# Attention with a gated feed-forward: half-swapped rows copied a block ahead on POOL's queue, work moved to ACT at the start, and a rebuilt last part

## The chip, the cores and the metric

The kernel runs on one core of one Trainium2 chip. Five engines work side by side, each through its own instructions in order: PE (TensorE, matrix products; its weight loads, PEld, overlap with them), DVE (VectorE), ACT (ScalarE), POOL (GpSimd) and SP (SyncE, which issues transfers). SBUF is the memory on the core with 128 partitions; PSUM holds the matrix products in banks of 128 x 512 f32. Transfers (DMA) are issued from the queue of SP, ACT or POOL. An instruction on one engine that needs another's result waits on a semaphore.

The metric is the time of one execution in microseconds (us) on the device; shown is the median of three runs.

## What is computed

The reference, cut to what matters:

```python
def reference(A_x, A_k_cache, A_v_cache, A_wq, A_wo, B_x, B_w1, B_w3, B_w2):
    # x: 1 x 2048 x 640; k, v: 1 x 32 x 2048 x 192 (32 heads); wq: 640 x 6144; wo: 6144 x 640
    xn = (x - mean(x)) / sqrt(var(x) + 1e-5)             # per row
    q = (xn @ wq).reshape(1, 2048, 32, 192).transpose(0, 2, 1, 3)
    p = softmax(einsum("bhqd,bhkd->bhqk", q, k) * 192 ** -0.5)
    s = einsum("bhqk,bhkd->bhqd", p, v).transpose(0, 2, 1, 3).reshape(1, 2048, 6144) @ wo
    h = silu(xn @ w1) * (xn @ w3)                        # w1, w3: 640 x 1536
    g = silu(h @ w2)                                     # w2: 1536 x 640
    return x + s * g
```

All inputs and the output are bf16.

## The kernel before

The 2048 rows of x are 16 tiles of 128 rows (`NQT`) and 4 query blocks of 512 (`NQB`, index `qb`). Each head has 16 key tiles of 128, taken as 8 pairs (`NPAIR`, index `p`).

**Norm.** `ln_stats(i)` makes mean and variance of tile i on DVE (two batch statistics and an aggregate). `ln_sums` does the same for tile 1 alone on ACT: two passes with accumulators and a small scaling. `ln_root(i0)` makes the reciprocal roots of two tiles on ACT, `ln_scale(i0)` applies them on DVE. `ln_turn` transposes a pair of tiles on PE into a bank (`pst`) and copies them into `xnT` (ACT; DVE for tiles 2 and 3). `xnT` holds the normed x with its 640 columns on 5 x 128 partitions.

**Swapped rows.** `xnS` holds the same rows with the halves of the 128 partitions swapped, so that a product can be cut into two products of 64 rows that use both halves of PE at once. `swap_rows(qb)` (line 290) fills 512 columns of it with two transfers of 320 KB from `xnT`, issued on ACT's queue. `project_chunk(h, qb)` (line 260) makes a block of queries for head h: for head 0 from `xnT` alone, for all others from `xnT` and `xnS`. Its 512 x 2 product is cast into `qA` and `qF` (`cast`, on DVE unless given), and POOL makes shifted copies `qS` and `qD`. The chunk also carries a slice of w1 or w3, whose results are taken up by `swiglu_chunk` for most of the feed-forward's hidden part.

**Attention.** `advance(hd, qb, p, extra)` does one step: `scores` (6 products into an `st2` bank pair of `ps_st`, which has two), `weights` (one exp on ACT, 128 x 1024, with a bound `nb` instead of the row maximum), and the products of earlier steps with the values (`parts`, kept three half-steps behind; four when `extra` is given). `extra` is other PE work put between. After the last pair, `evict` copies and adds the halves of an output bank (`osum`, DVE), and writes the scaled result to `ostage`; for the second bank this last step is put off into `late`, which the next `advance` empties. The banks `ob0` and `ob1` are one each, so the next block's products wait until `osum` has left them.

**Head 0** runs interleaved with the rest of the norm: `extras` puts the transposes of the next block's tiles, head 0's own next projection and head 1's projection of the present block between the steps, `posts` puts statistics, roots and scalings behind them. In blocks 1 to 3 `swap_rows(qb)` follows step 0, and head 1's projection of that block, which reads it, comes at step 6 (block 3: step 1). POOL's weights for head 2 are issued at the start of block 3. `next_bound(qb)` makes the bound of the coming block: small DVE operations and an all-reduce over the partitions on POOL.

**Heads 1 to 31** project the next head's block at step 1 of each block. Head 31 has no next head: there `extra` calls `ffn_hidden(0, qb)` (line 514), which makes 128 hidden columns for 512 rows: ten products into an `st2` bank pair, tanh of the gate on ACT (`t`), and on DVE `a` = (t+1) * gate and `hT` = a * up, where gate and up are read from the two halves of the bank pair.

**Last part.** Ahead of the last two value parts of head 31 stands `ffn_hidden(1, 0)`. Then, for each block, the remaining hidden columns and four `ffn_out` (product with w2, tanh, gate into `g_all`); `tail_ps` hands out banks for both, in turn from `ps_st` and from `ob0`/`ob1`. Last come 16 `output_tile`: 96 products of 320 columns with wo (48 for each of two pieces of 320), a multiplication (`tmp`) and the sum with x (`res`) on DVE for each piece, and one store on ACT's queue. Only in the last tile are the two pieces made one after the other, in two banks. A branch behind it repeats everything exactly if a bound failed; it isn't taken.

`pin` keeps instructions of an engine in the order of the program.

Of the kernel before, what the change touches and what calls it, by code (L numbers as in the profile page):

```python
# [9 lines left out]
ACT = mybir.ActivationFunctionType  # L10
# [6 lines left out]
P = 128  # L17
# [13 lines left out]
def _kernel_impl(ctx, tc, A_x, A_k_cache, A_v_cache, A_wq, A_wo, B_w1, B_w3, B_w2, out):  # L31
# [96 lines left out]
    with ExitStack() as actx:  # L128
# [26 lines left out]
        sums = lnx.tile([P, 1], F32, name="sums")  # L155
        sqs = lnx.tile([P, 1], F32, name="sqs")
        nmean = lnx.tile([P, 1], F32, name="nmean")
# [27 lines left out]
        def ln_sums(i):  # L185
            junk = lnp.tile([P, D], BF16, tag="junk", name="junk")
            pin(nc.scalar.activation(out=junk[:], in_=x_all[:, i, :], func=ACT.Identity, accum_out=sums[:]))
            pin(nc.scalar.mul(out=nmean[:], in_=sums[:], mul=-1.0 / D))
            pin(nc.scalar.activation(out=junk[:], in_=x_all[:, i, :], func=ACT.Square, bias=nmean[:], scale=1.0,
                                     accum_out=sqs[:]))  # L190
# [3 lines left out]
        def ln_root(i0):  # L194
            lv = lnp.tile([P, 2], F32, tag="lv", name="lv")
            if i0 == 0:
                pin(nc.scalar.activation(out=lv[:, 0:1], in_=mv[:, 0, 1:2], func=ACT.Ln, bias=eps_t[:], scale=1.0))
                pin(nc.scalar.activation(out=lv[:, 1:2], in_=sqs[:], func=ACT.Ln, bias=eps_t[:], scale=1.0 / D))
            else:
                pin(nc.scalar.activation(out=lv[:].unsqueeze(2), in_=mv[:, i0:i0 + 2, 1:2], func=ACT.Ln, bias=eps_t[:],  # L200
                                         scale=1.0))
            rstd[i0] = lnx.tile([P, 2], F32, name=f"rstd{i0}")
            pin(nc.scalar.activation(out=rstd[i0][:], in_=lv[:], func=ACT.Exp, scale=-0.5))
# [3 lines left out]
        def ln_scale(i0):  # L207
            scaled[i0] = []
            for t in range(2):
                i = i0 + t  # L210
                xn = xnp.tile([P, D], BF16, tag="xn", name="xn")
                act = i == 1
                pin(nc.vector.tensor_scalar(out=xn[:], in0=x_all[:, i, :], scalar1=nmean[:] if act else mv[:, i, 0:1],
# [76 lines left out]
        def swap_rows(qb):  # L290
            qs = slice(qb * 512, (qb + 1) * 512)
            for t in range(2):
                pin(nc.scalar.dma_start(out=xnS[ROWS[t], :, qs], in_=xnT[ROWS[1 - t], :, qs]))
# [142 lines left out]
        maxima = project_chunk(0, 0, nc.scalar.copy)  # L436
        swap_rows(0)
# [8 lines left out]
        ln_stats(4)  # L446
# [8 lines left out]
        def first_project(h, qb):  # L455
            project_chunk(h, qb)()
# [3 lines left out]
        def steps(*fs):  # L460
# [4 lines left out]
            (0, 2): ((ln_root, 6), (ln_scale, 6)),  # L465
            (0, 3): ((ln_stats, 8), (ln_stats, 9)),
# [7 lines left out]
        for qb in range(NQB):  # L474
# [8 lines left out]
            for p in range(NPAIR):  # L483
                advance(heads[0], qb, p, extras.get(p), early.pop(0) if early else None)
                if p == 0 and qb:
                    swap_rows(qb)
# [30 lines left out]
        def ffn_hidden(qb, fl, ps):  # L517
# [7 lines left out]
            pin(nc.scalar.activation(out=t[:], in_=ps[:, 0:512], func=ACT.Tanh, scale=0.5))  # L525
            a = fsb.tile([P, 512], BF16, tag="a", name="a")
            pin(nc.vector.scalar_tensor_tensor(out=a[:], in0=t[:], scalar=1.0, in1=ps[:, 0:512], op0=ALU.add, op1=ALU.mult))  # L527
            pin(nc.vector.tensor_tensor(out=hT[:, FCP + fl, :], in0=a[:], in1=ps[:, 512:1024], op=ALU.mult))  # L528

        for h in range(1, H):  # L530
# [10 lines left out]
            for qb in range(NQB):  # L541
                post = []

                def extra():
# [5 lines left out]
                    else:  # L550
                        ffn_hidden(0, qb, ps_st.tile([P, 1024], F32, tag="st2", name="ps_gu"))
# [20 lines left out]
        def tail_ps(name):  # L572
            turn[0] += 1
            if turn[0] % 2:
                return ps_st.tile([P, 1024], F32, tag="st2", name=name)
            return ps_o.tile([P, 2, 512], F32, tag=f"ob{turn[0] // 2 % 2}", name=name)[:].rearrange("p t c -> p (t c)")
# [5 lines left out]
        ffn_hidden(1, 0, ps_st.tile([P, 1024], F32, tag="st2", name="ps_gu"))  # L582
        load_hT(1)
        while parts:
            parts.pop(0)()
        late.pop(0)()
# [18 lines left out]
    def output_tile(pools, i, oT, xt):  # L605
# [3 lines left out]
        pieces = [(ps_s[-pi if split else 0][:, pi * 512:pi * 512 + c1 - c0], c0, c1) for pi, (c0, c1) in enumerate(DP)]  # L609
# [10 lines left out]
        nc.scalar.dma_start(out=out2[i * P:(i + 1) * P, :], in_=res[:])  # L620
# [16 lines left out]
    with ExitStack() as dctx:  # L637
# [5 lines left out]
        for qb in range(NQB):  # L643
            if qb + 1 < NQB:
                for fl in range(1 if qb == 0 else 0, FC - FCP):
                    ffn_hidden(qb + 1, fl, tail_ps("ps_gu"))
# [139 lines left out]
```

## Time and profile before

| | |
|---|---|
| runs | 1965.85, 1967.06, 1969.59 us; median 1967.06 |
| the profiled execution | 1967.95 us; its span, first to last instruction, 1966.1 us |
| granted TensorE clock, mean over the span | 0.996 |
| DMA: queue of SP (q1), of ACT (q10), of POOL (q0) | 27.9%, 1.7%, 5.1% of 16 engines' span |
| exp of one step (L369, ACT) | 1016 + 8 of 1114 ns |
| query casts on DVE (L277, L278) / on ACT (head 0's first) | 691 and 681 ns / 585 and 592 ns |
| copy of a transposed tile (L222, ACT) | 694 ns |
| gate and product in `ffn_hidden` (L527, L528, DVE) | 687 and 687 ns |
| swap transfers (L293, ACT's queue) | 8 of 320 KB, median 5.5 us to landing |
| store of a result tile (L620, ACT's queue) | 16 of 160 KB, median 8.7 us to landing, 1.8 at least |

How to read it: a busy time is the sum of an engine's instructions; PE's products overlap one another a little in these records. A wait is time in which an engine stood idle before an instruction, put down to what ended it. A line of the timeline gives start, duration, engine, line, operation, output <- inputs, shapes, count, and in brackets the idle time before it with what ended it. "Landing" is when a transfer's semaphore is complete, counted from the start of its issue.

### The profile page before, as it was taken

The numbers are of one execution on the slowest core, as the hardware profiler recorded it, in microseconds if no ns is written. First come the engines' busy times: TensorE is split into PE (matmuls) and PEld (weight loads), VectorE is DVE, ScalarE is ACT, GpSimd is POOL, SyncE is SP. The second block draws the span as 40 slices with busy tenths as digits, with TensorE's granted clock in tenths as the row PEclk, the third lists the DMA queues.
The fourth block names the chain that finished last, engine by engine and source line by source line (L and its number), as shares of the span: only waits on it lengthen the run. The fifth ranks groups of instructions, "written<-read, shape, count | busy, mean of one in ns | idle before, by whom it ended". The sixth has DMA issues, their size and how long they took to land.

```text
span 1966.1 us, 60463 instructions
## 1 busy us (share of the span) xinstructions
PE 1940.3 (99%) x27233; PEld 1422.1 (72%) x27233; DVE 1140.2 (58%) x2256; ACT 1213.7 (62%) x1176; POOL 435.5 (22%) x632
## 2 busy tenths in 40 slices
PE   8899999999999999999999999999999999999998
PEld 4577777777777777777777766666666666567776
DVE  7666667666666666666666666666666653421111
ACT  5577767677777777777777777777777777210000
POOL 2322222222222222222222222222222110000000
PEclk9999999999999999999999999999999999999999
DMA  9322323222233322232323232323232112927882
GB/s 207 64 68 48 68 53 69 58 62 64 62 68 62 68 62 68 54 88 68 75 54 76 54 76 48 82 46 84 46 84 46 39 42 84 269 58 139 154 155 51
DMA packets 354681, 153.51 MB, mean 78 GB/s; under 512 B 303648, under 2 KB 348160, under 8 KB 354416
## 3 DMA queue, kind: packets, MB, share of 16 engines
q1 hardware_dynamic: 337200, 117.82, 27.9%
q0 software_dynamic: 8032, 23.93, 5.1%
q10 hardware_dynamic: 9184, 7.83, 1.7%
q8 instruction: 215, 3.52, 0.8%
q14 instruction: 50, 0.41, 0.1%
HBM read 56.23 MB, written 31.98 MB: 45 GB/s over the span
## 4 chain that ended last, share of the span: by engine, by line
PE 96%; DVE 2%; DMA 1%; ACT 0%; issue 0%; POOL 0%; SPq 0%; ACTq 0%
PE obank L409 34%; PE st L363 33%; PE ps L275 14%; PE ps_s L612 11%; PE ps_f L628 3%; PE ps_gu L522 2%; PE ps L269 0%; DVE st L182 0%; DMA xnS<-xnT 0%; DVE st L286 0%; ACT pT L369 0%; DMA x_all<-in_A_x_dram 0%; DVE a L527 0%; DVE hT L528 0%; DVE osum L380 0%
## 5 line engine op out<-in xcount | busy, mean ns | idle before, releaser
L369 ACT ACTIVATE pT<-st,nb 128x1024 bf16<-128x1024 f32 x1016 | 1131.4, 1114 | 455.7 <-PE st L363 454.1
L409 PEld LDWEIGHTS <-pT 64*128 64x128 bf16 x16384 | 762.5, 94 | 196.0 <-DVE osum L380 2.5
L409 PE MATMUL obank<-vt,pT 64*128 64x193 bf16 x16384 | 876.9, 243 | 2.6 <-DVE osum L380 2.1
L379 DVE COPY osum<-obank 128x386 f32<-128x386 f32 x256 | 142.5, 556 | 506.5 <-PE obank L409 506.5
L363 PE MATMUL st<-qA,KA 64*128 64x512 bf16 x2048 | 415.3, 376 | 4.7 <-ACT pT L369 2.5
L363 PE MATMUL st<-qS,KB 64*128 64x512 bf16 x1024 | 385.2, 376 | 0.3 <-POOL qS L281 0.3
L363 PE MATMUL st<-qS,KC 64*128 64x512 bf16 x1024 | 385.0, 376 | 0.3 <-POOL qS L281 0.3
L363 PE MATMUL st<-qD,KC 64*128 64x512 bf16 x1024 | 385.0, 376 | 0.3 <-POOL qD L282 0.3
L363 PE MATMUL st<-qF,KB 64*128 64x512 bf16 x1024 | 385.0, 376 | 0.0
L281 POOL COPY qS<-qA 64x512 bf16<-64x512 bf16 x256 | 190.9, 746 | 604.4 <-DVE qA L277 595.5
L275 PE MATMUL ps<-xnT,wq 64*128 64x512 bf16 x1240 | 292.2, 378 | 0.0
L275 PE MATMUL ps<-xnS,wq 64*128 64x512 bf16 x1240 | 284.7, 378 | 5.8 <-DMA xnS<-xnT 5.8
L363 PEld LDWEIGHTS <-KC 64*128 64x128 bf16 x2048 | 191.9, 94 | 97.1 <-issue 1.4
L275 PEld LDWEIGHTS <-wq 64*128 64x128 bf16 x2480 | 146.7, 94 | 100.8 <-issue 8.1
L612 PE MATMUL ps_s<-wo_sb,oT 128*128 128x320 bf16 x1536 | 208.8, 299 | 0.0
L363 PEld LDWEIGHTS <-KB 64*128 64x128 bf16 x2048 | 192.5, 94 | 13.2 <-issue 0.8
L612 PEld LDWEIGHTS <-oT 128*128 128x128 bf16 x1536 | 150.3, 98 | 58.3
L386 DVE TENSOR_TENSOR ostage<-osum,rl_all 128x384 bf16<-128x384 f32 x256 | 149.6, 584 | 8.8
L380 DVE TENSOR_TENSOR osum<-osum,obank 128x386 f32<-128x386 f32 x256 | 142.6, 557 | 8.9
L363 PEld LDWEIGHTS <-KA 64*128 64x128 bf16 x2048 | 126.8, 94 | 21.0 <-issue 8.8
L617 DVE SCALAR_TENSOR_TENSOR tmp<-ps_s,g_all 128x320 f32<-128x320 f32 x32 | 15.6, 488 | 176.4 <-PE ps_s L612 176.4
L277 DVE CAST qA<-ps 128x512 bf16<-128x512 f32 x127 | 87.8, 691 | 37.7 <-PE ps L275 13.6
(85 smaller groups left out, 1175.4 us busy)
## 6 DMA issues: line engine op xcount, KB each, us to landing
vt<-in_A_v_cache_dram SPq DMA_DIRECT2D x32, 768.0 KB, 6.4
o_scr<-ostage SPq DMA_DIRECT2D x64, 384.0 KB, 2.9
wo_sb<-in_A_wo_dram POOLq DMA_DIRECT2D x1, 7680.0 KB, 33.1
wq<-in_A_wq_dram POOLq DMA_DIRECT2D x31, 160.0 KB, 3.0
hT_scr<-hblk SPq DMA_DIRECT2D x16, 256.0 KB, 2.9
xnS<-xnT ACTq DMA_DIRECT2D x8, 320.0 KB, 5.5
xt<-in_A_x_dram POOLq DMA_DIRECT2D x16, 160.0 KB, 9.5
out_dram<-res ACTq DMA_DIRECT2D x16, 160.0 KB, 8.7
```

Source lines behind the costliest of these rows:

```text
L275: pin(nc.tensor.matmul(ps[:, t * 512:(t + 1) * 512], lhsT=wq[ROWS[t], s, :], rhs=xs[ROWS[t], s // 2, qs], start=(s == 0), stop=(s == 2 * D ...
L277: pin(cast(out=qA[:, qs], in_=ps[:, 0:512]))
L281: keep(nc.gpsimd.tensor_copy(out=qS[ROWS[t], qs], in_=qA[ROWS[1 - t], qs]))
L363: pin(nc.tensor.matmul(st2[:, t * 512:(t + 1) * 512], lhsT=k[ROWS[t], ks], rhs=q[ROWS[t], qs], start=(s == 0), stop=(s == 2)))
L369: pin(nc.scalar.activation(out=pT2[:], in_=st2[:], func=ACT.Exp, scale=SCALE, bias=nb[:]))
L379: pin(nc.vector.tensor_copy(out=osum[:], in_=ov[:, 0, :, 0:DH + 1]))
L380: pin(nc.vector.tensor_tensor(out=osum[:], in0=osum[:], in1=ov[:, 1, :, 0:DH + 1], op=ALU.add))
L386: pin(nc.vector.tensor_tensor(out=ostage[:, b * 2:b * 2 + 2, hg * DH:(hg + 1) * DH], in0=osum[:, :, 0:DH], in1=rl.unsqueeze(2).to_broadcas ...
L409: pin(nc.tensor.matmul(acc["o"][b][:, r, (j % 2) * 256:(j % 2) * 256 + DH + 1], lhsT=pT2[ROWS[r], t * 512 + j * P:t * 512 + (j + 1) * P], ...
L522: pin(nc.tensor.matmul(ps[:, o:o + 512], lhsT=w_sb[:, c, fl * P:(fl + 1) * P], rhs=xnT[:, c, qs], start=(c == 0), stop=(c == DC - 1)))
L612: pin(nc.tensor.matmul(ps, lhsT=oT[:, k, :], rhs=wo_sb[:, k, c0:c1], start=(k == 0), stop=(k == OC - 1)))
L628: pin(nc.tensor.matmul(ps[:, pi * 512:pi * 512 + c1 - c0], lhsT=hT[:, fc, qsl], rhs=w2_sb[:, fc, c0:c1], start=(fc == 0), stop=(fc == FC - ...
```

## The change

In the start:

- `swap_rows` issues on POOL's queue. Block 0 is swapped where it was in the program; blocks 1 to 3 are swapped one block ahead, behind step 5 of block 0 and step 4 of blocks 1 and 2.
- The statistics of tile 4 move from DVE (`ln_stats(4)`) to ACT (`ln_sums(4)`, behind head 0's first casts); the sums have two columns now, and `ln_root` takes the logarithm of the pair 4, 5 in two instructions.
- `ln_root(6)` and `ln_scale(6)` come behind step 3 of block 0 instead of step 2.
- Head 1's four projections are cast by ACT instead of DVE.

In `ffn_hidden`: DVE first copies the up half of the bank pair to SBUF (`u`, bf16); the product `hT` = a * u is returned as a function. Head 31 calls it from `late`, behind the put-off eviction; the one ahead of the last two value parts is called behind them; the others at once.

In the last part: `tail_ps` gives the second tail tile a bank pair of `ps_st` instead of `ob1`, and from there on even turns `ps_st`, odd turns `ob0` and `ob1` in turn. The last output tile is cut into 512 and 128 columns instead of 320 and 320, and each piece is stored by itself.

```diff
+        ASUM = {1: 0, 4: 1}
...
         def ln_sums(i):
+            k = slice(ASUM[i], ASUM[i] + 1)
...
-            pin(nc.scalar.activation(out=junk[:], in_=x_all[:, i, :], func=ACT.Identity, accum_out=sums[:]))
+            pin(nc.scalar.activation(out=junk[:], in_=x_all[:, i, :], func=ACT.Identity, accum_out=sums[:, k]))
...
         def ln_root(i0):
-            if i0 == 0:
...
+            if i0 in ASUM or i0 + 1 in ASUM:
+                for t in range(2):
+                    i = i0 + t
+                    if i in ASUM:
+                        pin(nc.scalar.activation(out=lv[:, t:t + 1], in_=sqs[:, ASUM[i]:ASUM[i] + 1], func=ACT.Ln, bias=eps_t[:],
+                                                 scale=1.0 / D))
+                    else:
+                        pin(nc.scalar.activation(out=lv[:, t:t + 1], in_=mv[:, i, 1:2], func=ACT.Ln, bias=eps_t[:], scale=1.0))
...
         def swap_rows(qb):
...
-                pin(nc.scalar.dma_start(out=xnS[ROWS[t], :, qs], in_=xnT[ROWS[1 - t], :, qs]))
+                pin(nc.gpsimd.dma_start(out=xnS[ROWS[t], :, qs], in_=xnT[ROWS[1 - t], :, qs]))
...
         maxima = project_chunk(0, 0, nc.scalar.copy)
+        ln_sums(4)
         swap_rows(0)
...
-        ln_stats(4)
         ln_stats(5)
...
         def first_project(h, qb):
-            project_chunk(h, qb)()
+            project_chunk(h, qb, nc.vector.tensor_copy if h == 0 else nc.scalar.copy)()
...
-            (0, 2): ((ln_root, 6), (ln_scale, 6)),
-            (0, 3): ((ln_stats, 8), (ln_stats, 9)),
+            (0, 3): ((ln_root, 6), (ln_scale, 6), (ln_stats, 8), (ln_stats, 9)),
...
                 advance(heads[0], qb, p, extras.get(p), early.pop(0) if early else None)
-                if p == 0 and qb:
-                    swap_rows(qb)
+                if p == (4 if qb else 5) and more:
+                    swap_rows(qb + 1)
...
             pin(nc.scalar.activation(out=t[:], in_=ps[:, 0:512], func=ACT.Tanh, scale=0.5))
+            u = fsb.tile([P, 512], BF16, tag="u", name="u")
+            pin(nc.vector.tensor_copy(out=u[:], in_=ps[:, 512:1024]))
             a = fsb.tile([P, 512], BF16, tag="a", name="a")
             pin(nc.vector.scalar_tensor_tensor(out=a[:], in0=t[:], scalar=1.0, in1=ps[:, 0:512], op0=ALU.add, op1=ALU.mult))
-            pin(nc.vector.tensor_tensor(out=hT[:, FCP + fl, :], in0=a[:], in1=ps[:, 512:1024], op=ALU.mult))
+            return lambda: pin(nc.vector.tensor_tensor(out=hT[:, FCP + fl, :], in0=a[:], in1=u[:], op=ALU.mult))
...
-                        ffn_hidden(0, qb, ps_st.tile([P, 1024], F32, tag="st2", name="ps_gu"))
+                        late.append(ffn_hidden(0, qb, ps_st.tile([P, 1024], F32, tag="st2", name="ps_gu")))
...
             turn[0] += 1
-            if turn[0] % 2:
+            if turn[0] == 1 or turn[0] % 2 == 0:
                 return ps_st.tile([P, 1024], F32, tag="st2", name=name)
-            return ps_o.tile([P, 2, 512], F32, tag=f"ob{turn[0] // 2 % 2}", name=name)[:].rearrange("p t c -> p (t c)")
+            return ps_o.tile([P, 2, 512], F32, tag=f"ob{(turn[0] // 2 + 1) % 2}", name=name)[:].rearrange("p t c -> p (t c)")
...
-        ffn_hidden(1, 0, ps_st.tile([P, 1024], F32, tag="st2", name="ps_gu"))
+        rest = ffn_hidden(1, 0, ps_st.tile([P, 1024], F32, tag="st2", name="ps_gu"))
         load_hT(1)
         while parts:
             parts.pop(0)()
+        rest()
         late.pop(0)()
...
-        pieces = [(ps_s[-pi if split else 0][:, pi * 512:pi * 512 + c1 - c0], c0, c1) for pi, (c0, c1) in enumerate(DP)]
+        pieces = [(ps_s[-pi if split else 0][:, pi * 512:pi * 512 + c1 - c0], c0, c1)
+                  for pi, (c0, c1) in enumerate(((0, 512), (512, D)) if split else DP)]
...
-        nc.scalar.dma_start(out=out2[i * P:(i + 1) * P, :], in_=res[:])
+            if split:
+                nc.scalar.dma_start(out=out2[i * P:(i + 1) * P, c0:c1], in_=res[:, c0:c1])
+        if not split:
+            nc.scalar.dma_start(out=out2[i * P:(i + 1) * P, :], in_=res[:])
...
-                    ffn_hidden(qb + 1, fl, tail_ps("ps_gu"))
+                    ffn_hidden(qb + 1, fl, tail_ps("ps_gu"))()
```

## The prediction

> **What bounds the kernel now.** I read the page's busy times, the chain of waits, PE's waits, the stretches around the two long ones, and the timeline.
>
> ```profile
> span 1966.1 us, 60463 instructions
> PE 1940.3 (99%) x27233; PEld 1422.1 (72%) x27233; DVE 1140.2 (58%) x2256; ACT 1213.7 (62%) x1176; POOL 435.5 (22%) x632
> PE 96%; DVE 2%; DMA 1%; ACT 0%; issue 0%; POOL 0%; SPq 0%; ACTq 0%
> ```
>
> PE is the bound: 1940.3 of 1966.1 us. Heads 1 to 30 run the same instructions in the same order on every engine in both kernels, and PE's waits below all lie before 81 us or after 1616. So the change can only move the 25.8 us in which PE stands still, and stretches in which PE is busy but slow. PE's waits over the span, the largest:
>
> ```profile
> PE ps L275 <- DMA xnS<-xnT: 5.8, 1, 5.8
> PE st L363 <- ACT pT L369: 2.5, 4, 1.7
> PE obank L409 <- DVE osum L380: 2.1, 2, 1.5
> PE ps_gu L522 <- DVE osum L380: 2.0, 1, 2.0
> PE st L363 <- DVE hT L528: 1.5, 4, 0.4
> ```
>
> (us in total, times, longest.) The stretches (us, then busy time of PE, PEld, DVE, ACT, POOL; granted clock; DMA share; GB/s) show a second cost behind two of these waits:
>
> ```profile
> 75.00:80.00 5.00, 0.00 (x0) 0.00 (x0) 2.85 (x6) 1.11 (x1) 2.84 (x4) 0.81 0.78 161
> 80.00:85.00 5.00, 4.73 (x24) 1.98 (x25) 0.27 (x1) 0.00 (x0) 0.01 (x1) 0.51 0.00 0
> 1672.00:1676.00 4.00, 1.98 (x9) 0.72 (x8) 3.79 (x9) 0.60 (x1) 0.00 (x0) 0.94 0.00 0
> 1675.50:1680.00 4.50, 4.50 (x14) 1.71 (x15) 1.99 (x4) 0.45 (x1) 0.00 (x0) 0.62 0.62 135
> ```
>
> After the 5.8 us wait PE runs at half clock up to 84.9; after the 2.0 us wait it does so too, from 1675.5 on. The 1.7 us wait (at 21.9) and the 1.5 us one (at 39.3) show no such drop.
>
> **(a) Swapped rows one block earlier, on POOL's queue.** Before, block 3's swap is issued on ACT at 73.41 and PE wants it at 74.3:
>
> ```profile
> 68.73 0.38 POOL L322 PARTITION_ALL_REDUCE nb<-ns  x1 [0.55 <-DVE ns L319]
> 71.20 1.27 POOL L281 COPY qS<-qA 64x512 bf16<-64x512 bf16 x2 [2.09 <-DVE qA L277]
> 73.41 1.79 ACTq L293 DMA_DIRECT2D xnS<-xnT  x1
> 80.27 0.61 PE L275 MATMUL ps<-xnS,wq 64*128 64x512 bf16 x2 [5.79 <-DMA xnS<-xnT]
> ```
>
> The wait costs 5.8 us. The half clock from 80.27 to 84.9 costs half of 4.6, so 2.3; together 8.1. In the new POOL order block 3's two transfers stand right behind the all-reduce that ends at 69.11, in the 2.09 us where POOL idled. An issue on POOL takes 0.72 to 1.04 us (rows of wq), so the two take about 1.5 and qS waits at most 0.1 longer; behind qS stand qD, weights and KC of later heads, not wanted before 88. In the other blocks KC or qS of head 1 stand behind the swap, wanted no sooner. Queue SP's order is unchanged, and ACT loses eight issues. Landing is not shown for this copy on this queue. The same copy on ACT's queue, alone at 54.8, landed its halves 3.6 and 4.6 us after issue: 69.85+4.6 = 74.45 against 74.3. Loads on POOL's queue took 2.4 to 3.0 alone, 4.7 to 5.7 beside the swap at 73, and 10.3 to 10.8 in the crowded start. So 0 to 6 us of waiting remain; I take 0.4, because the stretch 69 to 74 moves only 3 GB/s and resembles 54.8 most. Gain 7.7.
> Blocks 1 and 2 have over 9 us between landing and use. Block 0 goes from ACT (12.79) to POOL behind qD (15.3), ahead of head 1's weights, and is wanted near 31.7. Those weights, issued at 15.24, landed 10.5 us later; up to 22.3 the DMA view lists 0.65 MB of the swap's queue and no packet of POOL's. That same 0.65 MB now precedes the weights in POOL's own queue, so I expect them at 27.3 as before and cost it at nothing; at the 0.33 MB per 3.4 us that POOL's queue made from 22.3, both would land near 33, a wait of 1.5.
> The row: the 62 wq issues of POOL average 737 ns against 716 at best, though DVE is 58% busy. The Trainium skill (SBUF — State Buffer, section "SBUF: two separate sides") warns that a DMA from the GpSimd queue can stall while DVE holds the shared port in a two-port mode, and sends such transfers to ACT or SP; by that rule the two issues could be stretched, which is the first rival. That row does not bear it out.
>
> **(b) Tile 4's statistics on ACT, head 1's first casts on ACT, root 6 one step later.** Tile 4's sums take 2.02 us on ACT (4.04 to 6.06 for tile 1). x tile 4 lands at 14.2 (issue 8.84, 5.4 us), so ACT ends at 16.3, before the first exp at 17.21: hidden, margin 0.9.
>
> ```profile
> 23.58 0.39 PE L363 MATMUL st<-qA,KA 64*128 64x512 bf16 x2 [1.73 <-ACT pT L369]
> ...
> 40.86 1.01 PE L409 MATMUL obank<-vt,pT 64*128 64x193 bf16 x20 [1.52 <-DVE osum L380]
> ```
>
> DVE loses two batch statistics and an aggregate, 1.1 us. Before, exp 3 stood behind root 6, which waited for DVE until 22.00, and PE idled 1.7. Now exp 3 starts near 20.9, but two copies (1.3) and the root (0.5) come before exp 4, and the transposes of tile 6 wait for its rstd until 24.35 instead of 25.00: 0.65 gained. The three-instruction root instead of two costs ACT 0.2, hidden.
> Head 1's casts leave DVE (0.69+0.68) and cost ACT 1.07 a time. ACT idled 2.0 before the next exp in these steps, so that exp slips 0.3 and PE, three half-steps ahead, does not see it. DVE reaches the eviction of the finished block 0.5 earlier. At 37.6 PE gains that; the 1.5 us osum wait at 40.86 moves with it and stays (bounds of the whole 0 to 1.8). I take 1.0. At 58.8 a wait of 0.5 shrinks, while exp at 57.3 may slip 0.1: 0.3 (bounds -0.3 to 0.8).
>
> **(c) ffn_hidden with the copy u.** In head 31 PE's four 0.37 us waits are for hT, the second reader of the bank: t 0.60, a 0.69, hT 0.69 in a row. Now u (0.69, as a cast of 512) runs beside t, and the bank is free after a: 0.6 us earlier. All four go: 1.5.
>
> **(d) Tail order.**
>
> ```profile
> 1675.50 6.17 PE L522 MATMUL ps_gu<-xnT,w_sb 128*128 128x512 bf16 x20 [2.02 <-DVE osum L380]
> ```
>
> The second tail tile now takes the st2 bank that ffn_hidden(1,0) frees near 1671.95 instead of ob1, free at 1675.46. PE wants it at 1673.4: 2.0 gained, and the half clock: 20 matmuls took 6.17 us where 40 take 8.7 later, so 1.8. DVE adds u but hT from SBUF should fall toward 0.42 (hblk row), some 1.8 a chunk against PE's 2.16. The next st2 bank is freed near 1677.55, wanted at 1677.8: narrow. Gain 3.85 (0 to 3.9).
>
> **(e) Last tile 512+128.**
>
> ```profile
> 1959.87 0.49 DVE L617 SCALAR_TENSOR_TENSOR tmp<-ps_s,g_all 128x320 f32<-128x320 f32 x1 [5.50 <-PE ps_s L612]
> 1960.40 0.49 DVE L619 TENSOR_TENSOR res<-tmp,xt 128x320 bf16<-128x320 f32 x1
> 1960.92 0.34 ACTq L620 DMA_DIRECT2D out_dram<-res  x1
> ```
>
> Matmuls: 48 of 512 columns at 0.215 (L522) and 48 of 128 at 0.057 (transposes of L221: 10 in 0.73, less one's 0.22, over 9) make 13.07 against 13.04; were each held by its 98 ns weight load, +2.0. DVE: 320 columns 0.49, 512 columns 0.69, so 128 take 0.29: -0.4. The store landed 3.4 us after issue, others of its size in 1.8 at best; a fifth of the bytes: -0.4 (0 to -1.6). Gain 0.8 (-1.6 to 2).
>
> **Sum.** 7.7+1.0+0.3+1.5+3.85+0.8 = 15.15 us. The profiled execution took 1967.95 (1.85 around its span) and becomes 1952.8; the median shown, 1967.06, lies 0.9 lower, so 1952.
>
> **Rivals.**
> 1. The swap of block 3 still comes late. If each issue on POOL is held by one DVE cast (0.69), or first packets start 1.2 later as beside other traffic (4.7 against 3.6 landed), 2 us of waiting return, and with them a half-clock stretch like the tail's 1.8: 1952+1.6+1.8 = 1955.5. For: 74.45 against 74.3 is no margin. Against: little other traffic then.
> 2. Block 0 and head 1's weights land near 33: 1.5 lost, 1953.5; with half clock 1955.5.
> 3. The tail's wait turns into one for DVE: nothing of (d) is gained, 1955.9. For: margin 0.25. Against: PE would wait for only one a, 0.7.
> 4. Other residual waits near 1.7 us lose the clock. The drop lasted 3.4 us after 2.0 us of idling and 6.8 after 5.8. The Trainium skill (TensorE: Matmul & The Clock Gate, section "What's actually happening") has a free-running window of about 3.4 us, with half rate after an idle one; the trace agrees with the length, but shows a drop after 2.0 us. So the osum wait near 39.7 could cost 1.7: 1953.7.
> 5. Slower: POOL's queue serves its five transfers of the start one after another, each with the 5.7 us beyond the usual that its first showed (7.1 to the first packet against 1.4). Head 1's last weights then land near 45 against 31.7: 13 lost, 2.3 of clock, and (a) is lost too, 8: 1976. It decides from 15 us lost. Against: the three landed within 2.2 us of each other.
>
> **Chances.** Forecast 0.55 (own range 1949.5 to 1954.5); rival 1 0.15, rival 2 0.08, rival 3 0.08, rival 4 0.06, rival 5 0.06, nothing net 0.02. Within 0.2% (3.9 us, what a measurement can tell) lies only the last. Range 1947.5 to 1958.5: the lower end is (b) and (e) at their good bounds, the upper rivals 1 and 3 together. Faster 0.92, same 0.02, slower 0.06.
>
> **What would show it.** PE's wait for xnS under 0.5 us and a clock of 1.00 from 72 to 90; no PE wait for hT in head 31; no PE wait for osum and clock 1.00 near 1672; DVE's last two at 0.29. A wait for xnS or wq above 2 us, or one for `a` in the tail, makes me wrong.

## The result, and where the time went

The changed kernel takes 1961.05 us (median of 7 runs, 1956.17 to 1963.59), the kernel before 1967.78 in the same set (1965.56 to 1971.42): ratio 0.996, 95% interval 0.9947 to 0.9973. By the medians it is faster by 6.7 us and not by the 15.15 forecast, and it lies 2.55 us above the range. The execution whose profile is shown next took 1956.17 and is the fastest of the seven; the page's span, busy times and chain:

```profile
span 1954.4 us, 60484 instructions
PE 1938.0 (99%) x27233; PEld 1329.0 (68%) x27233; DVE 1139.2 (58%) x2261; ACT 1219.5 (62%) x1190; POOL 439.5 (22%) x640
PE 97%; DVE 1%; DMA 1%; ACT 0%; POOL 0%; issue 0%; DVEq 0%
```

PE is still the bound. Its waits (us in total, times, longest):

```profile
PE pst L228 <- DVE xn L220: 2.8, 3, 1.9
PE obank L416 <- DVE osum L387: 2.1, 3, 1.5
...
PE st L370 <- DVE a L535: 1.0, 4, 0.3
```

Gone are the 5.8 us for the swapped rows, the 1.7 at 21.9 and the tail's 2.0. The four waits of head 31 are still there, 0.25 each in place of 0.37. The stretches that answer to those of before (PE, PEld, DVE, ACT, POOL; granted clock; DMA share; GB/s):

```profile
75.00:80.00 5.00, 4.78 (x60) 2.70 (x56) 4.80 (x9) 3.07 (x4) 4.84 (x8) 1.00 0.35 76
80.00:85.00 5.00, 5.00 (x88) 3.74 (x86) 3.86 (x10) 4.08 (x4) 2.91 (x5) 1.00 0.22 58
...
1664.50:1671.00 6.50, 6.50 (x34) 2.96 (x31) 6.27 (x14) 1.19 (x2) 0.00 (x0) 1.00 0.05 15
```

PE works through both places at full clock. I compared the start times of the same products in both traces, group by group. Of the 11.7 us by which this span is shorter, 7.7 come between 68 and 100 us (block 3's swap), 0.65 from the first block, 0.5 from head 31, 3.87 from the second tail tile, 1.17 from the end. 1.5 are lost again before 12 us (a half clock from 7.7 to 11.1 us that the profile of before does not have) and 0.8 in small steps between 100 and 1610 us; I have no cause for the latter.

So this one execution has nearly all that was forecast. What the other six lost, 3 to 7 us, is not in it. Two more executions of the same kernel show it, in the first experiment.

### The profile page after: what moved, and what is told of

Same layout as the page of the kernel before. It is cut to its first block, busy times and chain, and to the rows that moved or that the text cites. A ratio compares the mean times of both kernels' runs of the same rounds, so it can differ in the third digit from the quotient of the medians.

```text
span 1954.4 us, 60484 instructions
## 1 busy us (share of the span) xinstructions
PE 1938.0 (99%) x27233; PEld 1329.0 (68%) x27233; DVE 1139.2 (58%) x2261; ACT 1219.5 (62%) x1190; POOL 439.5 (22%) x640
## 4 chain that ended last, share of the span: by engine, by line
PE 97%; DVE 1%; DMA 1%; ACT 0%; POOL 0%; issue 0%; DVEq 0%
PE obank L416 34%; PE st L370 33%; PE ps L282 14%; PE ps_s L622 11%; PE ps_f L641 3%; PE ps_gu L528 2%; DMA wq<-in_A_wq_dram 1%; PE ps L276 0%; DVE st L293 0%; DVE osum L387 0%; DMA x_all<-in_A_x_dram 0%; DVE osum L386 0%; DVE xn L220 0%; DVE u L533 0%; DVE ostage L393 0%
## 5 line engine op out<-in xcount | busy, mean ns | idle before, releaser
L416 PEld LDWEIGHTS <-pT 64*128 64x128 bf16 x16384 | 718.4, 94 | 240.4 <-DVE osum L387 2.8
L416 PE MATMUL obank<-vt,pT 64*128 64x193 bf16 x16384 | 855.2, 243 | 2.6 <-DVE osum L387 2.1
L370 PE MATMUL st<-qA,KA 64*128 64x512 bf16 x2048 | 392.5, 376 | 2.7 <-DVE a L535 1.0
L622 PE MATMUL ps_s<-wo_sb,oT 128*128 128x320 bf16 (+2 forms) x1536 | 208.8, 299 | 0.0
L282 PEld LDWEIGHTS <-wq 64*128 64x128 bf16 x2480 | 122.5, 94 | 115.3 <-DMA wq<-in_B_w_dram 0.6
L370 PEld LDWEIGHTS <-KA 64*128 64x128 bf16 x2048 | 104.9, 93 | 21.7 <-issue 6.7
L627 DVE SCALAR_TENSOR_TENSOR tmp<-ps_s,g_all 128x320 f32<-128x320 f32 (+2 forms) x32 | 15.6, 487 | 176.1 <-PE ps_s L622 176.1
L99 POOL DMA_DIRECT2D wq<-in_A_wq_dram x62 | 45.2, 730 | 278.0 <-PE ps L282 265.8
```

Of the source, the lines that this page charges most:

```text
L99: keep(nc.gpsimd.dma_start(out=wq[ROWS[t], :, c0:c1], in_=w.rearrange("(s p) d -> p s d", p=DT)))
L282: pin(nc.tensor.matmul(ps[:, t * 512:(t + 1) * 512], lhsT=wq[ROWS[t], s, :], rhs=xs[ROWS[t], s // 2, qs], start=(s == 0), stop=(s == 2 * D ...
L370: pin(nc.tensor.matmul(st2[:, t * 512:(t + 1) * 512], lhsT=k[ROWS[t], ks], rhs=q[ROWS[t], qs], start=(s == 0), stop=(s == 2)))
L416: pin(nc.tensor.matmul(acc["o"][b][:, r, (j % 2) * 256:(j % 2) * 256 + DH + 1], lhsT=pT2[ROWS[r], t * 512 + j * P:t * 512 + (j + 1) * P], ...
L622: pin(nc.tensor.matmul(ps, lhsT=oT[:, k, :], rhs=wo_sb[:, k, c0:c1], start=(k == 0), stop=(k == OC - 1)))
```

## Experiments

Every time is the median of its runs; "before" is the kernel before in the same set (1967.2 to 1967.8 in all sets).

**The change once more, twice (look_a, look_b).** No edit.

> The changed kernel again, for a second profile: its seven times spread from 1956.17 to 1963.59 us and the profiled one was the lowest. Theory: in the profiled one PE reached head 1's first projection late, because a half-clock stretch at 7.7 to 11.1 us had cost it 1.5 us, and so it waited only 0.2 us for head 1's weights, which land near 33 us behind the swap of block 0 in POOL's queue. In a run without that stretch PE comes at about 31.2 us and waits 1.5 to 2.5 us there, with a half-clock stretch behind the wait: span 1957 to 1960. Rival: no wait above 0.5 us there, and the time is lost in half-clock stretches that follow no such wait.

> The same kernel a third time; the same two expectations as for the second look. If the theory holds, the wait for weights or swapped rows near 32 us grows by as much as PE comes earlier, in each of the looks.

Measured: 1960.94 and 1964.35. All their loss against the profile above arises between 27 and 43 us (5.8 and 9.5 us in the start times of the products); behind it the three executions keep their distance. PE's timeline of look_a there:

```profile
31.09 0.24 PE L416 MATMUL obank<-vt,pT 64*128 64x193 bf16 x1
35.12 0.80 PE L416 MATMUL obank<-vt,pT 64*128 64x193 bf16 x7 [3.78 <-issue]
```

PE stops for 3.78 us behind the first of eight equal value products, and the releaser is "issue": nothing that the profile shows held it. Its inputs come from the same two tiles as those of the product before it. The stretches of look_a show what follows:

```profile
30.00:35.00 5.00, 1.33 (x23) 0.74 (x18) 3.73 (x11) 1.88 (x2) 3.48 (x6) 0.91 1.23 92
35.00:40.00 5.00, 4.88 (x29) 3.43 (x30) 0.00 (x0) 0.00 (x0) 1.03 (x1) 0.50 1.14 239
```

The clock is half in the second line. The DMA engines are taken all the time (share above 1) and yet move only 92 GB/s in the first. Look_a has no wait for head 1's weights: the theory had the place and the half clock, but not the cause. Look_b stops at the same product for 1.7 us and then does wait for them, by more than the 2 us that the prediction named as a sign of being wrong:

```profile
PE ps L282 <- DMA wq<-in_A_wq_dram: 5.5, 2, 4.9
PE obank L416 <- issue: 1.7, 1, 1.7
```

**Block 0's swap back on ACT, at its new place (swap0_act), and the early swaps alone (only_swap).**

The first edits the change, the second the kernel before (`swap_rows` takes the engine as an argument in the first):

```diff
-        swap_rows(0)
+        swap_rows(0, nc.scalar)
```
```diff
-                pin(nc.scalar.dma_start(out=xnS[ROWS[t], :, qs], in_=xnT[ROWS[1 - t], :, qs]))
+                pin(nc.gpsimd.dma_start(out=xnS[ROWS[t], :, qs], in_=xnT[ROWS[1 - t], :, qs]))
...
-                if p == 0 and qb:
-                    swap_rows(qb)
+                if p == (4 if qb else 5) and more:
+                    swap_rows(qb + 1)
```

> The changed kernel with block 0's swap alone issued on ACT's queue again. Theory (head 1's weights stand behind the swap in POOL's queue): the weights land near 27 us as before the change, PE does not wait near 32 us, and the median falls 3 to 5 us under the changed kernel's 1961.05, to 1956 to 1958 us. Rival (the spread comes from the clock alone, in the start or the tail): no gain, 1960 to 1962 us.

> The kernel before with the swap alone changed: POOL's queue, one block ahead. Theory: the wait at 74 us and its half clock go, 7.8 us, and a wait of 1 to 2 us for head 1's weights near 32 us is added, with or without 1.7 us of half clock: 1960.5 to 1963 us. Rival (no cost at 32 us): 1959 to 1960.5 us. Rival (the gain at 74 us is given back later): above 1964 us.

Measured: swap0_act 1955.61 (1954.94 to 1961.09), ratio 0.9943 (0.993 to 0.9956); only_swap 1964.63 (1961.34 to 1971.57), ratio 0.9992 (0.998 to 1.0003).

Swap0_act's median is even a little under what was expected, but not for the reason given: in its profile (1959.42) head 1's weights land at 33.0 to 35.1 us and not near 27. Its five times fall into two groups, 1954.94 to 1955.61 (three) and 1959.42 and 1961.09. So with the swap late but on ACT's queue most of the loss is absent in three executions of five; none of these was profiled, and why is open.

Only_swap is the part of the change that was to bring 7.7 us. Made alone it brings 3.0 by the medians, and the interval of its ratio includes no gain at all. Its profile gains 7.3 us between 68 and 100 us and has lost 5.4 between 31 and 38.

Both profiled executions have the stop, 2.2 and 3.3 us at the same product, and a half clock behind it; in swap0_act too, although its swap is not on POOL's queue. What the two share with the change is the late issue of block 0's swap: 16.5 us on ACT, since it now stands behind tile 4's statistics, 15.4 to 16.7 on POOL, where it stands behind the copies of head 0's queries; before, 12.8.

**What PE waits for.** Queue q8 ("instruction" in the page's list of queues) carries packets of 16 KB. The table gives, for each profiled execution, when block 0's swap and head 1's first key transposes were issued, the first such packet of the trace (the expectation of act_early calls it the second), and the product at which PE stopped, the second of those eight (us, worked out from the traces' records):

```
                 swap issued    keys    q8 packet      product   behind its  PE stood
                 (queue)        issued  from - to      starts    landing     still
before           12.8 (ACT)     15.9    23.27-24.54    31.77      7.2        -
the change       16.7 (POOL)    15.1    28.88-30.82    32.38      1.56       -
look_a           15.4 (POOL)    15.7    32.68-33.72    35.12      1.40       3.8
look_b           15.4 (POOL)    15.4    29.65-31.53    33.02      1.49       1.7
swap0_act        16.5 (ACT)     15.4    32.52-33.57    35.00      1.43       2.2
only_swap        15.5 (POOL)    15.2    32.88-34.00    35.49      1.50       3.3
before_pool0     15.7 (POOL)    16.2    32.23-34.20    35.59      1.39       3.1
keys_wait        17.1 (POOL)    15.6    33.96-34.99    36.27      1.28       2.4
act_early        12.9 (ACT)     16.8    24.20-25.48    31.95      6.5        -
swap0_sp         15.4 (SP)      16.9    27.99-29.00    32.65      3.6        -
pool_early       12.0 (POOL)    16.6    28.01-29.02    35.63      6.6        -
keys_wait2       15.5 (POOL)    25.6    24.00-25.21    31.10      5.9        -
act_early_junk   13.1 (ACT)     16.2    24.36-25.64    31.23      5.6        -
```

In every execution that stops, the product starts 1.3 to 1.5 us after that packet has landed; where the packet is earlier, nothing stops. The three other profiled executions (no_u, no_b, fills14, below) agree: landed 3.2 to 7.9 us ahead of the product, no stop. I read this as PE running out of program: the packet brings its next instructions. The trace does not name the engine a packet is for, so this is inferred. The counts support it: before has 215 such packets for 27,233 products and as many weight loads of PE, 253 for each packet, and from the start of one packet to that of the next PE begins 258 instructions in the median (256 in the change), although the time between two varies from 3.1 to 24.8 us. All other engines together have some 6,000 instructions. The change's own profile just escaped, by about 0.1 us; its early half clock had made PE late.

**When block 0's swap is issued (act_early, pool_early, swap0_sp), and the late swap alone (before_pool0).**

The first three edit the change: swap on ACT ahead of tile 4's statistics, on POOL ahead of POOL's copies, on SP ahead of head 1's keys.

```diff
+        swap_rows(0, nc.scalar)
         ln_sums(4)
-        swap_rows(0)
```
```diff
+        swap_rows(0)
         maxima = project_chunk(0, 0, nc.scalar.copy)
         ln_sums(4)
-        swap_rows(0)
```
```diff
-        swap_rows(0)
+        swap_rows(0, nc.sync)
```

The fourth is the kernel before with this one swap on POOL's queue:

```diff
-        swap_rows(0)
+        swap_rows(0, nc.gpsimd)
```

> Edit to the changed kernel: block 0's swap goes back to ACT's queue and stands there ahead of tile 4's statistics, as in the kernel before; the other swaps stay ahead on POOL's queue. T (the moment of block 0's swap): in before it was issued at 12.8 and 13.5 us, ahead of SP's transposes of head 1's keys (15.9); in the change at 16.7, behind them (15.1), and in the run with it on ACT behind the statistics at 16.5. From then to 33 us swap, head 1's weights, the transposes and the 16 KB packets of queue q8 (instruction) share the DMA engines; where PE's second q8 packet began at 32.5 to 32.9 (23.3 in before), PE stood still 2.2 to 3.8 us from 31.3 to 32.8 and went on 1.4 to 1.5 us after the packet had landed. By T this run issues the swap before 14.5, the q8 packet begins before 27, no idle time of PE put down to issue above 0.5 us and no half clock between 30 and 45 us; median 1954 to 1956. Rival Q (POOL's descriptor queue itself): the same time as T, but the packet's start follows the queue, which pool_early tells. Rival O (tile 4's statistics and the casts, whatever the swap): stall of 2 us or more near 32 stays, median 1959 to 1962.

> Edit: block 0's swap stays on POOL's queue but is put ahead of POOL's copies of qA and qF, so that it waits for xnT alone and not for ACT's casts. T: issue near 12 us in place of 16.7, ahead of the key transposes, so no stall near 31 us and median 1954 to 1956, as act_early. Q (the queue, not the moment): the swap still lands after 27 us, weights after 32, a stall of 2 to 4 us at 31 us or a wait for wq above 1 us, median 1959 to 1962. O: as the change, 1959 to 1962, whatever the swap's landing.

> Edit: block 0's swap on SP's queue, ahead of head 1's key transposes, which then can't pass it; all else as the change. T (what stands ahead of the swap decides): issued near 15 us behind x_all, landing before 22, q8 packet before 27, no stall near 31 us, median 1954 to 1957; head 1's weights land before 30. Q: also fast (not on POOL). O: stall stays, 1959 to 1962. If the stall stays although the swap has landed before 22 us, T falls.

> Edit to the kernel before, one step alone: only block 0's swap goes to POOL's queue (behind POOL's copies); all other swaps stay on ACT where they were. T: the swap is issued near 15.2 in place of 12.8, level with or behind the key transposes (15.9 in before), and the crowd of 20 to 33 us comes: q8 packet after 28, PE's stall near 31 us and half clock after it, 3 to 6 us slower than before (ratio 1.0015 to 1.003). O: no change (ratio 1.000). What the loss would be if only the later weights mattered: below 1.5 us, a wait for wq at 33 us without a stall put down to issue.

Measured: act_early 1954.69 (1954.61 to 1956.11), ratio 0.9935 (0.9922 to 0.9948); pool_early 1958.99, 0.9955 (0.9942 to 0.9969); swap0_sp 1954.78, 0.9932 (0.9919 to 0.9945); before_pool0 1973.71 (1967.66 to 1975.46), 1.0024 (1.0011 to 1.0037). By the medians, moving this one transfer costs the kernel before 5.9 us, and moving it back gives the change 6.4. The statistics and casts (O) have nothing to do with it. Act_early's stretches at the place:

```profile
30.00:35.00 5.00, 5.00 (x70) 2.99 (x66) 4.59 (x12) 2.58 (x3) 3.78 (x7) 1.00 1.19 249
35.00:40.00 5.00, 4.08 (x62) 2.53 (x56) 4.60 (x9) 4.53 (x9) 4.03 (x6) 1.00 1.38 104
```

Pool_early has no stop at 31 us either, so POOL's queue alone is not what stops PE; it loses elsewhere:

```profile
PE obank L416 <- DMA vt<-in_A_v_cache_dram: 3.1, 1, 3.1
```

The swap, issued at 12.0, now shares the DMA engines with head 0's values, which land 11.4 us after their issue in place of 7.8 in the change: too early is dear as well. One point of T failed: swap0_sp's q8 packet came at 28.0 and not before 27, without harm.

**Whether the key transposes do it (keys_wait, keys_wait2).** Block 0's swap stays where the change put it; SP reads a few columns of the swapped rows first, so that head 1's key transposes begin only when they have landed.

```diff
-        loads[1] = {**load_weights(1), **load_keys(1)}
+        loads[1] = load_weights(1)
+        gate = lnx.tile([P, 8], BF16, name="gate")
+        for t in range(2):
+            pin(nc.sync.dma_start(out=gate[ROWS[t], :], in_=xnS[ROWS[t], 0, 0:8]))
+        loads[1].update(load_keys(1))
```

> Edit to the changed kernel: block 0's swap stays where the change put it (POOL's queue, behind POOL's copies, issue near 16 us), but SP reads 8 columns of each half of xnS's block 0 into a small tile before head 1's key transposes, so that these begin only when the swap has landed. Theory M (row copies and key transposes mixed on the DMA engines crawl: 60 to 330 of the transposes' 256-byte packets per us in the runs with the stall, 1,000 to 1,130 when they run alone in before): the swap lands before 25 us, head 1's weights before 29, transposes then run at about 1,000 packets per us, the q8 packet begins before 29, no idle time of PE put down to issue above 0.5 us at 31 to 35 us; median 1954 to 1957. Rival Q (POOL's queue is itself slow, 14.3 us to landing in the change): swap lands after 28, keys of head 1 then land after 45, stall or wait for wq near 32 stays; 1959 to 1963. Rival P (the issue's moment alone, after 15.5 us, whatever runs beside it): as Q in time.

> As keys_wait, but with SP's order now held: in keys_wait the two small reads of xnS came behind head 1's key transposes on SP's queue (35.5 us against 15.6 and 22.8), so these did not wait and the run only repeated the change (stall 2.4 us before 36.3). Here the reads stand ahead of the transposes. Theory M (row copies and key transposes mixed on the DMA engines hold each other up, and PE's program with them): swap issued near 17 on POOL's queue lands before 25 us, weights before 29, transposes then run alone at about 1,000 packets of 256 bytes per us, no stall put down to issue above 0.5 us at 31 to 36 us; median 1954 to 1957. Rivals Q (POOL's queue itself slow) and P (the issue's moment alone): swap lands after 28, stall or wait for wq stays, 1959 to 1963.

Keys_wait missed its aim: the reads were issued at 35.5 us, behind the transposes, and the run repeats the change (1962.03, ratio 0.9976, 0.9967 to 0.9985). In keys_wait2 the transposes and the values' load of head 1 are held in program order too, and the reads come first: 1955.02 (1954.44 to 1955.9), ratio 0.9935 (0.9921 to 0.9948). Queue, place and moment of the swap are those of the change (15.45 us, as in look_a and look_b); apart from the two small reads, only the transposes moved. The DMA view from 11.5 to 21 us, of before, of the change, and of keys_wait2 (KB each, median us from issue to landing):

```profile
x_all<-in_A_x_dram SPq DMA_DIRECT2D x2, 640.0 KB, 13.2
xnS<-xnT ACTq DMA_DIRECT2D x2, 320.0 KB, 8.6
wq<-in_A_wq_dram POOLq DMA_DIRECT2D x1, 160.0 KB, 10.5
```
```profile
x_all<-in_A_x_dram SPq DMA_DIRECT2D x2, 640.0 KB, 7.9
xnS<-xnT POOLq DMA_DIRECT2D x2, 320.0 KB, 14.3
wq<-in_A_wq_dram POOLq DMA_DIRECT2D x1, 160.0 KB, 14.1
```
```profile
x_all<-in_A_x_dram SPq DMA_DIRECT2D x2, 640.0 KB, 9.7
xnS<-xnT POOLq DMA_DIRECT2D x2, 320.0 KB, 8.2
wq<-in_A_wq_dram POOLq DMA_DIRECT2D x1, 160.0 KB, 8.3
```

Before, the swap ran beside the loads of x and slowed them to 13.2 us; the key transposes stand behind these on SP's queue, so they came last, from 24 us on, and ran almost alone. In the change the loads of x have the engines for themselves (7.9), the transposes follow at 19 and meet the swap and head 1's weights, which take 14 us in place of 8 to 10.5. Packets of 256 bytes, the transposes', per us: 59 to 152 from 22 to 31 us in the change, beside the row copies; over 1,040 at the best in keys_wait2, alone.

**The load without a reader (act_early_junk).** Act_early, and where the change had the swap, POOL copies the same 320 KB again, to columns that block 3's swap writes over later.

```diff
         ln_sums(4)
+        for t in range(2):
+            pin(nc.gpsimd.dma_start(out=xnS[ROWS[t], :, 3 * 512:SQ], in_=xnT[ROWS[1 - t], :, 0:512]))
```

> Edit to act_early (1954.69): where the change had block 0's swap on POOL's queue, POOL now copies the same 320 KB a second time, into the columns of xnS that block 3's swap writes over later; nobody reads this copy before that, and block 0's own swap has gone early on ACT. By M the load alone brings the loss back: q8 packet after 28 us, PE standing still 2 to 4 us near 31 to 33 put down to issue, or weights of head 1 late, median 1958 to 1961. If PE stood still in the change because it waited for the swapped rows themselves (data late, not the program), this run stays at 1954 to 1955.5 apart from a wait for wq.

Measured: 1954.68 (1954.52 to 1955.36), ratio 0.9934 (0.9921 to 0.9948): no loss. My expectation failed. The early swap slowed the loads of x again, so the transposes reached the engines only from 25 us on, and the q8 packet had gone by at 24.4. Behind it the crowd did come: 4 to 374 packets of the transposes per us from 25 to 31 us, and head 1's weights landed at 30.3 to 31.1, just before PE needed them. So neither more bytes nor the crowd alone costs time here; by the reading above, the costly case is the crowd with that packet still to come. This run does not tell whether late rows alone would have stopped PE; against that stands only that the product at which PE stopped reads none of them. A copy without a reader that meets the transposes ahead of the packet wasn't tried.

**The other steps (no_u, no_b, fills14),** each against act_early, 1954.69:

```diff
-            u = fsb.tile([P, 512], BF16, tag="u", name="u")
-            pin(nc.vector.tensor_copy(out=u[:], in_=ps[:, 512:1024]))
...
-            return lambda: pin(nc.vector.tensor_tensor(out=hT[:, FCP + fl, :], in0=a[:], in1=u[:], op=ALU.mult))
+            pin(nc.vector.tensor_tensor(out=hT[:, FCP + fl, :], in0=a[:], in1=ps[:, 512:1024], op=ALU.mult))
+            return lambda: None
```
```diff
-        ln_sums(4)
...
+        ln_stats(4)
...
-            project_chunk(h, qb, nc.vector.tensor_copy if h == 0 else nc.scalar.copy)()
+            project_chunk(h, qb)()
...
-            (0, 3): ((ln_root, 6), (ln_scale, 6), (ln_stats, 8), (ln_stats, 9)),
+            (0, 2): ((ln_root, 6), (ln_scale, 6)),
+            (0, 3): ((ln_stats, 8), (ln_stats, 9)),
```
```diff
-        keep_busy(12)
+        keep_busy(14)
```

> Edit to act_early: ffn_hidden's copy u is taken out, and the product reads the second half of the PSUM tile again, as in the kernel before. By the prediction's step (c) u is worth 1.5 us (the four waits of 0.37 gone). By the trace of the change u runs behind t and not beside it (t 1612.6, u 1613.2), and the waits are 0.25: worth 0.5 us. So this run is slower than act_early by 0.5 (median near 1955.2) by the trace, by 1.5 (1956.2) by the prediction; the four waits of PE for DVE behind ps_gu go from 0.25 back to 0.37.

> Edit to act_early: the change's part in the first block is undone (tile 4's statistics back on DVE by bn_stats, head 1's first casts back on DVE, the roots and scales of tiles 6 and 7 back behind pair 2); swaps, u, tail and end as in act_early. The prediction's step (b) was 1.3 us; the marks of act_early show only 0.1 gained by 68 us over before (0.85 at the transposes of tiles 6 and 7, given back around them by half clock from 16.0 to 19.4 us). By the prediction: 1.3 slower than act_early (1956.0). By the marks: 0 to 0.9 slower (1954.7 to 1955.6), the wait of 1.5 to 1.7 us before the scores at 22 us back again.

> Edit to act_early: 14 fills in place of 12 at the start of PE, so that PE's idle time between the fills' end (5.7 to 6.9 us) and the first transposes (7.5 to 8.2) closes. If the early half clock (7.7 to 11.1 us in the change, 16.0 to 19.4 in act_early) comes of that idle time, it goes and the run is 0.5 to 1.5 us faster (1953.2 to 1954.2). If it comes of the waits at 12 to 16 us, no change (1954.7). If two more fills end after the first tiles are ready (at half clock 0.43 us each), up to 0.5 slower.

Measured: no_u 1956.73 (1955.77 to 1958.8), ratio 0.9946 (0.9932 to 0.9959); no_b 1957.46 (1956.23 to 1958.56), 0.995 (0.9936 to 0.9963); fills14 1954.73 (1954.14 to 1957.86), 0.9939 (0.9925 to 0.9952).

No_u's median is 2.0 slower, nearer to the prediction's 1.5 than to the trace's 0.5, but its profile doesn't put that down to u. The profiled execution (1958.8) is the slowest of the five, 4.1 slower than act_early's: 1.8 of that is there before 27 us (a half clock from 7.9 to 11.3 us) and 1.9 comes behind DVE's last instruction; u is in neither place. At the four waits it loses 0.12 to 0.13 each, 0.5 together, as the trace had said. The change's timeline shows why u gives so little (start, duration; idle before):

```profile
1612.61 0.60 ACT L531 ACTIVATE t<-ps_gu 128x512 bf16<-128x512 f32 x1 [0.38 <-PE ps_gu L528]
...
1613.24 0.69 DVE L533 CAST u<-ps_gu 128x512 bf16<-128x512 f32 x1 [0.86 <-ACT t L531]
1613.84 0.68 DVE L535 SCALAR_TENSOR_TENSOR a<-t,ps_gu 128x512 bf16<-128x512 bf16 x1
```

DVE stands idle until ACT's t is done, though u does not read t: both read the same PSUM tile, and the program built from the kernel makes the second reader wait for the first. So u, which was to run beside t, stands in the row t, u, a where hT stood. The two halves in tiles of their own weren't tried.

No_b is 2.8 slower by the medians. The 1.7 us wait for the exp near 22 us is back. In the start times of the two profiles it is 0.55 later at 22 us (half clock from 15.5 to 18.9, which act_early has at 16.0 to 19.4), 1.4 behind the transposes of tiles 6 and 7 at 25, 1.9 at 38 and 2.2 at 60. So 1.6 of it arises where the step works, of which 0.5, at 38 us, also differs between executions that share the step (next section). Fills14 keeps its half clock (16.7 to 20.2) and gains nothing, so the idle time ahead of the first transposes isn't its cause.

## Why the prediction was wrong

**(a), the early swaps: right where it was costed, wrong where it was "costed at nothing".** PE's wait for block 3's rows and the half clock behind it are gone: 7.7 us between 68 and 100 us against 7.7. The step that failed is the other half: "that same 0.65 MB now precedes the weights in POOL's own queue, so I expect them at 27.3 as before and cost it at nothing". The weights landed at 32 to 39 us, and the step costs 5.9 us alone (before_pool0) and 6.4 in the change (1961.05 against act_early's 1954.69). I had asked what stands behind the swap on POOL's queue and not what its absence on ACT's lets through on SP's: the loads of x speed up, the key transposes move ahead, and all three queues meet. Rival 2 had the place and the sign (0.08); its price of 1.5 us was for the data's lateness, while PE, by the reading above, stopped for its program, at a product that needed neither rows nor weights, with a half clock on top; only look_b waited for weights as well. Rival 5, POOL's queue serving its transfers slowly, falls: with the transposes out of the way it landed them after 8.2 us (keys_wait2).

**(b), the first block: 1.3 forecast.** Three pairs of profiles give 0.6 (act_early_junk against before, with a like early clock), 1.1 (act_early against before, its half clock left out) and 1.6 (no_b against act_early). All have 0.85 at the transposes of tiles 6 and 7, where 0.65 was put, and 0.25 near 60 us, where 0.3 was; at 38 us, where 0.35 more was expected, they differ from 0.5 lost to 0.5 gained. The 1.5 us wait for osum stayed, as said. The size stays open.

**(c), the copy u: 0.5 against 1.5.** The step "Now u (0.69, as a cast of 512) runs beside t" failed: u starts when t has ended, as shown above.

**(d), the tail's order: 3.87 against 3.85.** Wait and half clock are gone; the next wait, which the prediction called narrow, did not come. The match has some luck in it. Only_swap and before_pool0 still have the old tail and its 2.0 us wait, but their clock stays at 1.00 there. The two stretches that the prediction shows of before with 0.94 and 0.62, in only_swap:

```profile
1672.00:1676.00 4.00, 1.98 (x10) 0.80 (x9) 3.79 (x9) 0.60 (x1) 0.00 (x0) 1.00 0.00 0
1675.50:1680.00 4.50, 4.45 (x25) 2.38 (x25) 2.74 (x5) 1.20 (x2) 0.15 (x1) 1.00 0.95 209
```

So the wait is there in each of the three profiles, and its half clock, 1.7 us by the start times, in one.

**(e), the end: 1.2 against 0.8.** The products took as long as before (13.2 us), and DVE's last two came at the 0.29 forecast, 0.4 us gained as costed:

```profile
1949.34 0.29 DVE L627 SCALAR_TENSOR_TENSOR tmp<-ps_s,g_all 128x128 f32<-128x128 f32 x1 [1.26 <-PE ps_s L622]
1949.67 0.29 DVE L629 TENSOR_TENSOR res<-tmp,xt 128x128 bf16<-128x128 f32 x1
```

The other 0.75 is luck: the last store of before's profile landed 3.4 us after its issue, but the same uncut store took 2.15 in only_swap and before_pool0, and the smaller one of the change takes 1.9 to 2.3. So the 0.4 that the prediction gave to "a fifth of the bytes" is not there.

With block 0's swap early again the kernel gains 13.1 us (1967.8 to 1954.69) of the 15.15. From single profiles, 1.0 is missing at (c) and about 0.4 at (e); (b) and (d) vary too much between executions to be settled to a few tenths. Of the 9 us between forecast and result, some 6.4 are the one step costed at nothing. Act_early beats the change, which beats the kernel before; swap0_sp (1954.78) and keys_wait2 (1955.02) are level with it.

Some sums of the prediction do not come out as written: rivals 1 and 3 together make 1959.3 and not the range's 1958.5, (b) and (e) at their good bounds 1949.5 and not 1947.5, and rival 5 some 1975.3; its three loads landed within 1.6 us of each other (25.73 to 27.32) and not 2.2. The result lies outside the range so mended as well.

Rival 4 said that a wait near 1.7 us might lose the clock; no wait of that size did so by itself behind 16 us (look_b's 1.7 was followed at once by the wait for weights). Rivals 1 and 3 did not occur: no wait for the rows in block 3, none for DVE at the tail's first tiles.

## To carry to other kernels

A transfer that is moved off a queue also frees what it used to slow: before calling such a move free, list what stands on every queue at that moment and ask which transfer now gets ahead, above all transposes that will meet row copies. By the counts above PE's own program comes through the same DMA engines, so a stop with no releaser in the middle of a group of equal instructions is to be held against the instruction queue's packets. One profiled execution can be the lucky one: when a median is known, profile again until an execution near it is seen.

## What the runs showed of the hardware

Row copies and key transposes together are slower than one after the other. In keys_wait2, one after the other, head 1's weights had landed by 26.5 us and its key transposes by 34.2; together, by 33.2 and 34.9 in the change, 35.2 and 41.0 in look_a, 39.5 and 46.9 in look_b. In the change the transposes' packets fell to about a tenth, with a DMA share of 1.1 to 1.3 in each 5 us from 15 to 40 us. The 16 KB packet took 1.0 to 2.0 us itself, yet began up to 10.7 us later than in before. The Trainium skill (DMA: Bandwidth & Descriptors, section "Queues, rings and completion order") has each DMA engine go round the queues that have work, a packet at a time; a packet there is a group of descriptors, typically 9 to 17. By that rule alone the 16 KB packet would wait for one such group of each other busy queue. The trace shows when a packet starts and not when it was asked for, so the delay of 5 to 11 us (packets begun at 28.0 to 34.0 us against 23.3) is measured against other executions and its mechanism stays open.

The half clock comes in steps of 3.41 us, whose grid starts when the full clock was first granted, at 4.3 to 7.5 us, differently in each execution: look_a has the full clock from 6.79, half from 34.09, eight steps later, to 40.92, two more. Taking each trace's grid, of the steps behind 16 us all those at full clock in which PE idled 2.0 us or more were followed by a half-clock step (eight, 2.02 to 3.41 us), and none of the 21 with 1.2 to 1.9. That is why the stop's price varies: before_pool0's 3.1 us were cut by the grid into 1.89 and 1.23 and cost no clock, look_a's 3.8 cost two steps of it. It is also why the tail's 2.0 us cost the clock in before, where they lie in one step (1672.10 to 1675.52), and not in only_swap or before_pool0, where a border of the grid cuts them and no step idles more than 1.8. The Trainium skill (TensorE: Matmul & The Clock Gate, section "What's actually happening") has the free-running window of this length, and half rate after an idle one; here 2.02 us of idling in a window sufficed. Before 16 us the bound doesn't hold: 1.3 to 1.6 us in a step that began at 12 to 15 us lost the clock in six executions.
